# The last layer of an attention, expert and rational-layer kernel: its first products begun on two of three row tiles, and a fixed order of its instructions

## The chip, the cores and the metric

One core of one Trainium2 chip. The metric is the device time of one execution in microseconds. Before the change the median of 3 runs is 902.28 us (900.97 to 902.32).

## What is computed

Attention in which a query sees the keys of its own bucket, then a layer of 8 experts of which each token takes two, then a last layer with a rational activation:

```python
def _moe2_ref(x, w_in, w_out, a, b):      # x (1536, 512), w_in (512, 2048), w_out (2048, 512)
    h = x @ w_in
    h2 = h * h
    h3 = h2 * h
    P = a[0] + a[1] * h + a[2] * h2 + a[3] * h3
    Q = 1.0 + np.abs(b[0]) * np.abs(h) + np.abs(b[1]) * h2
    g = P / (Q + 1e-06)
    return (g @ w_out).astype(np.float32)
```

The change touches the last layer and its border to the last expert.

## The kernel before

The core's engines work from queues of their own: TensorE (PE) multiplies into PSUM, VectorE (DVE) and ScalarE (ACT) do the elementwise work and may read PSUM, GpSimd (POOL) works on SBUF alone and gathers rows by index, SyncE (SP) issues the other transfers. [...]

Each float32 factor is split in a high and a low part (fp32r), and a product is the sum of three terms: high x high, high x low, low x high.

**The last layer** (class `Last`) works through the 1536 tokens in 4 quarters of 384, each of three row tiles of 128 tokens. For each quarter there are 16 products f of 128 hidden columns, 64 in all, counted by q = 16 * quarter + f:
- `gather` (L1169) fetches a tile's two expert rows per token with two indexed transfers on GpSimd's queue; `combine` (L1178) adds them with their weights, one operation on ScalarE (L1180) and one on VectorE (L1181).
- `tr` (L1184) transposes the tile on TensorE (L1197) and splits it from PSUM into `x2T`: the high part on ScalarE (L1200), the low part on VectorE (L1201).
- `fc1` (L1203) is a first product: 12 matmuls (4 pieces of 128 rows by three terms) of 384 columns into one "ps1" bank (L1211).
- `first` (L1218): four ScalarE operations read the bank (L1222 to L1225: Abs into `ah`, the slope of Q into `qq`, a copy `hh`, the cubic term's start `uu`) and three VectorE operations work on those SBUF tiles (L1226 to L1228). `second` (L1230): 1/Q by Ln and Exp on ScalarE (L1233, L1234). `third` (L1236): three VectorE operations, a correction of 1/Q and the product with P (L1239 to L1241).
- `fourth` (L1243): the result is copied into the high half of `gT` by ScalarE (L1246) and GpSimd subtracts for the low half (L1247).
- `fc2` (L1250) is a second product: 9 matmuls of 512 columns (three terms by three row tiles) that add to three PSUM banks over a quarter's 16 values of f (L1263). Term (high, high) and the others come in the order term, row tile. At f = 15 the three banks are copied out (ScalarE L1274, VectorE L1272) and stored (L1276).

`run` (L1278) goes over steps s: first product s; `second` and `third` of s - 1; `fourth` and second product of s - 2; in the first three quarters the gathers of the next quarter's tiles at f = 4, 7, 10, and `combine` and `tr` two steps later; a weight split in every second step while weights are left (six of them). **The order** of the last layer's instructions on each engine is left to the scheduler of the framework, which uses its own estimates; the experts before it run in the order in which the program gives them (`manual_schedule`, for TensorE, ScalarE and VectorE).

`Weights.split` (L781) splits a weight tile of 1024 columns: high part on ScalarE (L793), low part on VectorE (L797); the next weight tile is then loaded on SP's queue.

**The border.** `Experts.run_last` (L1012) orders the last expert so that the rows of the first three tiles of the last layer can be gathered early, and does their `combine` and `tr` itself. Behind it stands `overflow_path` (L1104): all engines read a count and branch (L1108); the branch is not taken with these inputs. Only behind it do the first products of `Last.run` start, when all three tiles are there:

```python
        last.tr(1)
        for h in range(2):
            last.combine(2, slice(h * 256, h * 256 + 256))
        last.tr(2, 2)
```

Of the kernel before, what the change touches and what calls it, by code (L numbers as in the profile page):

```python
# [35 lines left out]
LONG = 3  # L36

# [702 lines left out]
class Weights:  # L740
# [5 lines left out]
    def __init__(self, tc, E):  # L746
        self.tc, self.nc, self.E = tc, tc.nc, E
        self.raw, self.slot = {}, {}
        self.ns = self.nl = 0
        self.ahead = 2  # L750
# [30 lines left out]
    def split(self, lo=None):  # L781
        nc, E = self.nc, self.E
        if self.ns >= 80:
            return
        n = self.ORDER[self.ns]
        self.ns += 1
        name = ("big1", "big2")[n // 8 % 2]
        pool = getattr(E, name)
        t = pool.tile([P, 2048], F32R, name=name, tag=name).rearrange("p (r s) -> p r s", r=2)
        self.slot[n] = t  # L790
        self.load()
        raw = self.raw.pop(n)
# [4 lines left out]
        (lo or nc.vector).tensor_tensor(t[:, 1, :], raw, t[:, 0, :].bitcast(F32), op=ALU.subtract)  # L797
        self.load()
# [59 lines left out]
class Experts:  # L858
# [153 lines left out]
    def run_last(self, last):  # L1012
# [3 lines left out]
        W = self.W  # L1016
# [26 lines left out]
        last.tr(0)  # L1043
# [60 lines left out]
def overflow_path(tc, E, last):  # L1104
# [3 lines left out]
    with tc.If(v > 0):  # L1108
# [3 lines left out]
        with tc.For_i(0, NE, 1) as e:  # L1112
            with tc.For_i(0, NTT, 1) as tt:
# [6 lines left out]
                ps = E.ps_1.tile([P, 512], F32, name="ps1")  # L1120
# [4 lines left out]
                for f in range(8):  # L1125
# [5 lines left out]
                    ph = E.ps_1.tile([P, 512], F32, name="ps1")  # L1131
# [22 lines left out]
        for tt in range(3):  # L1154
            last.gather(tt)
            last.combine(tt)
            last.tr(tt)


class Last:  # L1160
# [17 lines left out]
    def combine(self, tt, d=slice(0, DM)):  # L1178
        nc, E, t = self.nc, self.E, self.y[tt]
        nc.scalar.activation(t[:, 0, d], t[:, 0, d], AF.Copy, scale=E.gw[:, tt, 0:1])  # L1180
        nc.vector.scalar_tensor_tensor(t[:, 0, d], t[:, 1, d], E.gw[:, tt, 1:2], t[:, 0, d],  # L1181
                                       op0=ALU.mult, op1=ALU.add)

    def tr(self, tt, parts=1):  # L1184
# [6 lines left out]
        t, w = self.y[tt], 4 // parts  # L1191
        for h in range(parts):
            pool, name = ((E.ps_1, "ps1"), (E.ps_o, "o"))[(tt + h) % 2 if tt > 2 else 0]
            ps = pool.tile([P, 512], F32, name=name, tag=name)
# [8 lines left out]
    def fc1(self, q):  # L1203
# [4 lines left out]
        x = self.xT[ch]  # L1208
        ps = E.ps_1.tile([P, 512], F32, name="ps1")[:, 0:self.N]
        for n, (c, (a, b)) in enumerate([(c, t) for c in range(4) for t in ((0, 0), (0, 1), (1, 0))]):  # L1210
            nc.tensor.matmul(ps, w[:, a, c, fs], x[:, b, c, :], start=(n == 0), stop=(n == 11))  # L1211
        self.st[q] = {"ps": ps}
# [4 lines left out]

    def first(self, q):  # L1218
        nc, E, st = self.nc, self.E, self.st[q]
        ps = st.pop("ps")  # L1220
        ah, qq, u, h = (self.tmp(q, n, b) for n, b in (("ah", 1), ("qq", 2), ("uu", 2), ("hh", 1)))
        nc.scalar.activation(ah, ps, AF.Abs)  # L1222
        nc.scalar.activation(qq, ah, AF.Identity, scale=E.bb[:, 1:2], bias=E.bb[:, 0:1])  # L1223
        nc.scalar.activation(h, ps, AF.Copy)
        nc.scalar.activation(u, ps, AF.Identity, scale=E.na[:, 3:4], bias=E.na[:, 2:3])  # L1225
        nc.vector.tensor_mul(qq, qq, ah)  # L1226
        nc.vector.tensor_mul(u, u, h)  # L1227
        nc.vector.scalar_tensor_tensor(u, u, E.na[:, 1:2], h, op0=ALU.add, op1=ALU.mult)  # L1228

    def second(self, q):  # L1230
        nc, E, st = self.nc, self.E, self.st[q]
        r = self.tmp(q, "rr")
        nc.scalar.activation(r, st["qq"], AF.Ln, bias=E.c0)  # L1233
        nc.scalar.activation(r, r, AF.Exp, scale=-1.0)  # L1234
# [8 lines left out]
    def fourth(self, q):  # L1243
        nc, st = self.nc, self.st[q]
        g = self.pool.tile([P, 2, self.N], F32R, name="gT", bufs=2)
        nc.scalar.activation(g[:, 0, :], st["uu"], AF.Copy)  # L1246
        nc.gpsimd.tensor_tensor(g[:, 1, :], st["uu"], g[:, 0, :].bitcast(F32), op=ALU.subtract)  # L1247
        self.st[q] = g

    def fc2(self, q):  # L1250
# [9 lines left out]
        for a, b in ((0, 0), (0, 1), (1, 0)):  # L1260
            for j in range(3):
                ps = self.acc[ch][j]
                nc.tensor.matmul(ps, g[:, a, j * P:(j + 1) * P], w[:, b, f % 2, :],  # L1263
                                 start=(f == 0 and a + b == 0), stop=(f == 15 and a == 1))
# [13 lines left out]
    def run(self):  # L1278
        Q = 64
        for s in range(Q + 3):  # L1280
            ch, f = divmod(s, 16)
            if s < Q:
                self.fc1(s)
            if 0 <= s - 1 < Q:
                self.second(s - 1)
                self.third(s - 1)
            if 0 <= s - 2 < Q:
                self.fourth(s - 2)
            if s < Q:
                self.first(s)  # L1290
            if 0 <= s - 2 < Q:
                self.fc2(s - 2)
            if ch < 3:
                tt = 3 * (ch + 1)
                if f in (4, 7, 10):
                    self.gather(tt + (f - 4) // 3)
                if f in (6, 9, 12):
                    self.combine(tt + (f - 6) // 3)
                    self.tr(tt + (f - 6) // 3)
            if s % 2:  # L1300
                self.W.ahead = 2
                self.W.split()
# [3 lines left out]
def attention_moe_rational_kernel(ctx, tc, q, k, v, proj, w_gate, w_noise, noise, w1, w2, w_in, w_out, a, b, out):  # L1306
# [34 lines left out]
    with tc.tile_pool(name="big2", bufs=8) as E.big2, tc.tile_pool(name="xt", bufs=2) as E.xt:  # L1341
# [11 lines left out]
        with tc.tile_pool(name="fin", bufs=2) as last.pool:  # L1353
            last.run()
# [45 lines left out]
```

## Time and profile before

| what | value |
|---|---|
| median of 3 runs | 902.28 us |
| the profiled execution's own time | 905.34 us |
| its span (first to last instruction) | 903.6 us |
| TensorE busy | 863.3 us (96%) |
| VectorE busy | 747.9 us (83%) |
| ScalarE busy | 652.0 us (72%) |
| GpSimd busy | 357.8 us (40%) |
| mean granted TensorE clock | 0.986 |

The last expert ends, and the last layer starts, at about 604 us of the span. Busy time of TensorE is not TensorE at its peak: matmuls are pipelined, so the distance from one group's start to the next is what a group costs. A row of a timeline gives the start, the length, the engine, the line, the operation, the tiles out<-in, the shape, the count, and in brackets the idle time before it and what ended that. Some matmul records are missing from a trace, so counts can fall short.

### The profile page before, as it was taken

Reading aid. Unit: us, or ns where it says so; the run is one execution under the profiler, and the core shown is the slowest. Engines: PE = TensorE matmul, PEld = TensorE weight load, DVE = VectorE, ACT = ScalarE, POOL = GpSimd, SP = SyncE. Lnnn points to the kernel's source line nnn. Section 1 sums busy time; section 2 is a strip of 40 time slices with the busy share of each in tenths; the row PEclk is TensorE's granted clock in tenths of the full one; section 3 lists DMA queues with packets and bytes.
Section 4 is the critical chain, followed back from the end, with each engine's and each line's share of the span. In section 5 each row is a group of like instructions: output and inputs, shape, how many; then the busy total and the mean of one; then the engine's idle time right before and its main releaser. Section 6 shows DMA issues by size and latency. Waiting matters only on the chain. (4 is left out here: it accounts for less than half of the span.)

```text
span 903.6 us, 14378 instructions
## 1 busy us (share of the span) xinstructions
PE 863.3 (96%) x4673; PEld 769.6 (85%) x4673; DVE 747.9 (83%) x1450; ACT 652.0 (72%) x1272; POOL 357.8 (40%) x429
## 2 busy tenths in 40 slices
PE   7999999899998999999999999979999999999996
PEld 5999998799887888988998888868777999999895
DVE  6989999989896677867787667636999999999996
ACT  5898888788883555645656555527988988888885
POOL 5354445772465033534454343032672322222221
PEclk8999999999998999999999999998999999999999
DMA  6457776651152677797797877344231000000000
GB/s 203 115 129 202 207 204 192 179 174 32 50 198 102 187 234 251 262 292 258 267 325 227 281 235 252 128 123 148 82 91 32 30 12 27 10 1 19 18 1 35
DMA packets 90191, 131.39 MB, mean 145 GB/s; under 512 B 9248, under 2 KB 57376, under 8 KB 90112
## 3 DMA queue, kind: packets, MB, share of 16 engines
q1 hardware_dynamic: 86224, 117.72, 42.3%
q0 software_dynamic: 3888, 12.72, 4.3%
q8 instruction: 38, 0.62, 0.3%
q14 instruction: 41, 0.34, 0.1%
HBM read 87.68 MB, written 33.55 MB: 134 GB/s over the span
## 5 line engine op out<-in xcount | busy, mean ns | idle before, releaser
L923 PE MATMUL ps<-xsT,big 128*128 128x448 f32 (+1 forms) x768 | 159.2, 356 | 0.1
L1263 PE MATMUL s<-big,gT 128*128 128x512 f32 x528 | 141.0, 398 | 8.7 <-ACT gT L1246 5.6
L1211 PE MATMUL ps<-x2T,big 128*128 128x384 f32 x768 | 147.3, 340 | 1.5 <-DVEq L1108 1.5
L923 PEld LDWEIGHTS ps<-xsT,big 128*128 128x128 f32 x768 | 139.2, 189 | 7.9 <-DVE xsT L885 0.2
L1247 POOL TENSOR_TENSOR gT<-uu,gT 128x384 fp32r<-128x384 f32 x64 | 72.8, 1138 | 180.3 <-ACT gT L1246 150.8
L1211 PEld LDWEIGHTS ps<-x2T,big 128*128 128x128 f32 x768 | 137.2, 190 | 6.6 <-ACTq L1108 1.9
L943 PE MATMUL s<-big,hT 128*128 128x512 f32 x569 | 141.5, 393 | 0.7 <-ACT hT L928 0.7
L1263 PEld LDWEIGHTS s<-big,gT 128*128 128x128 f32 x528 | 96.3, 188 | 33.6 <-ACT gT L1246 9.8
L943 PEld LDWEIGHTS s<-big,hT 128*128 128x128 f32 x569 | 106.5, 188 | 21.3 <-ACT hT L928 1.0
L797 DVE TENSOR_TENSOR big<-wraw,big 128x1024 fp32r<-128x1024 f32 x76 | 97.4, 1286 | 27.8 <-ACT big L793 27.6
L357 DVE TENSOR_TENSOR PT<-ps,PT 128x384 fp32r<-128x384 f32 x192 | 105.4, 551 | 14.6 <-ACT PT L352 13.8
L847 POOL TENSOR_SCALAR convok<-convok 128x512 f32<-128x512 f32 x32 | 59.6, 1862 | 139.5 <-ACT convok L846 128.9
L352 ACT ACTIVATE PT<-ps 128x384 fp32r<-128x384 f32 x192 | 88.2, 493 | 29.8 <-PE ps L346 28.7
L338 ACT ACTIVATE probs<-s,sb 128x768 f32<-128x768 f32 x96 | 95.5, 995 | 3.6 <-DVE sb L331 3.4
L323 DVE TENSOR_REDUCE s<-s 128x1 f32<-128x768 f32 x96 | 92.2, 961 | 6.4 <-PE s L313 6.0
L313 PE MATMUL s<-big,qT 128*128 128x384 f32 x384 | 92.7, 364 | 4.1 <-ACT probs L338 3.2
L346 PE MATMUL ps<-ident,probs 128*128 128x128 f32 x576 | 85.7, 277 | 7.9 <-DVE sb L330 3.5
L793 ACT ACTIVATE big<-wraw 128x1024 fp32r<-128x1024 f32 x80 | 84.2, 1056 | 7.2 <-DMA wraw<-in_moe_w_dram 7.0
L367 PE MATMUL o<-PT,vhl 128*128 128x384 f32 x384 | 86.0, 346 | 0.6 <-ACT oT L373 0.6
L346 PEld LDWEIGHTS ps<-ident,probs 128*128 128x128 f32 x576 | 67.9, 141 | 20.2 <-PE ps L346 5.4
L1228 DVE SCALAR_TENSOR_TENSOR uu<-uu,na,hh 128x384 f32<-128x384 f32 x64 | 74.5, 1165 | 1.9
L928 ACT ACTIVATE hT<-ps 128x384 fp32r<-128x384 f32 x82 | 33.8, 412 | 51.9 <-PE ps L923 30.1
(222 smaller groups left out, 1474.9 us busy)
## 6 DMA issues: line engine op xcount, KB each, us to landing
wraw<-in_moe_w_dram SPq DMA_DIRECT2D x64, 512.0 KB, 5.4
wraw<-in_moe_w_in_dram SPq DMA_DIRECT2D x16, 512.0 KB, 5.6
wraw<-in_moe_w_out_dram SPq DMA_DIRECT2D x16, 512.0 KB, 4.1
xs<-zero SPq DMA_DIRECT2D x14, 512.0 KB, 4.4
qraw<-in_q_dram SPq DMA_DIRECT2D x32, 192.0 KB, 3.9
y<-io SPq DMA_DIRECT2D x24, 256.0 KB, 4.4
kraw<-in_k_dram SPq DMA_DIRECT2D x15, 384.0 KB, 4.0
w_in<-conv SPq DMA_DIRECT2D x16, 256.0 KB, 3.2
```

The costliest lines, as they stand in the source:

```text
L313: nc.tensor.matmul(ps[:, c, 0:384], T[:, r, q], R[:, r, c * 384:(c + 1) * 384], start=(r == 1), stop=(r == 0))
L323: nc.vector.tensor_reduce(m, ps[:, :, 0:384], axis=AX.XY, op=ALU.max, negate=True)
L338: nc.scalar.activation(pt.rearrange("p (c k) -> p c k", c=2), ps[:, :, 0:384], AF.Exp, bias=sb[:, 1:2], scale=sb[:, 0:1], accum_out=st["su ...
L346: nc.tensor.transpose(ps[:, i * P:(i + 1) * P], self.S[u]["P"][i][:, kt * P:(kt + 1) * P], E.ident)
L352: nc.scalar.activation(t[:, 0, :], ps[:, 0:384], AF.Copy)
L357: nc.vector.tensor_tensor(t[:, 1, :], ps[:, 0:384], t[:, 0, :].bitcast(F32), op=ALU.subtract)
L367: nc.tensor.matmul(self.O[u][:, 0:384], self.K[b, h]["vhl"][:, kt, :], t[:, r, :], start=(kt == 0 and r == 0), stop=(kt == 5 and r == 1))
L797: (lo or nc.vector).tensor_tensor(t[:, 1, :], raw, t[:, 0, :].bitcast(F32), op=ALU.subtract)
L923: nc.tensor.matmul(ps[:, 0:rows(e)], w[:, a, c, fs], x[:, c, b, 0:rows(e)], start=(n == 0), stop=(n == 11))
L943: nc.tensor.matmul(self.acc[e][j], h[a][:, j * P:(j + 1) * P] if j < 3 else tail, w[:, b, :], start=(f == 0 and a + b == 0), stop=(f == 7 ...
L1211: nc.tensor.matmul(ps, w[:, a, c, fs], x[:, b, c, :], start=(n == 0), stop=(n == 11))
L1263: nc.tensor.matmul(ps, g[:, a, j * P:(j + 1) * P], w[:, b, f % 2, :], start=(f == 0 and a + b == 0), stop=(f == 15 and a == 1))
```

## The change

1. Three first products begin before the third tile is there. In `run_last`, behind the second tile's transposes, product 0 is computed for tile 0 and for tile 1 separately and product 1 for tiles 0 and 1; then come the third tile's transposes, then product 2 for tiles 0 and 1. Behind the branch, `run` adds the third tile's columns of products 0, 1 and 2.
2. The last layer has a fixed order on TensorE, ScalarE and VectorE (`manual_schedule`). In step s TensorE does first product s + 1 and second product s - 3; `gT` has four buffers instead of two.
3. The elementwise work is cut anew. ScalarE: Abs with the slope from PSUM (`square`), the cubic term's start from PSUM (`cube`), Abs of Q's part, Ln, Exp, Copy: six operations where there were seven; the copies `ah` and `hh` go. VectorE: six operations as before, of which three read the PSUM bank as one input (`sign`, and both of `first`).
4. The low half of `gT` of the very last product is computed on VectorE, not on GpSimd. Second products at f = 0 and f = 15 go row tile by row tile.
5. Gathers at f = 0, 4, 8, their `combine` two steps later, `tr` at f = 5, 9, 13; weight splits from step 3 on, the low half at the end of VectorE's step.

```diff
@@ run_last
-        last.tr(0)
+        last.tr(0, (E.ps_1, "ps1"))
         last.combine(1)
 ...
-        last.tr(1)
+        last.tr(1, (E.ps_o, "o"))
         for h in range(2):
             last.combine(2, slice(h * 256, h * 256 + 256))
-        last.tr(2, 2)
+        for part in last.PARTS[:3]:
+            last.fc1(*part)
+        last.tr(2, (E.ps_o, "o"), (E.ps_s, "s"))
+        for part in last.PARTS[3:]:
+            last.fc1(*part)
@@ class Last
+    PARTS = (0, 0, 1), (0, 1, 2), (1, 0, 2), (2, 0, 2)
+    def fc1(self, q, i=0, j=3):
 ...
+        x, ps, n = self.xT[ch], self.st[q]["ps"], slice(i * P, j * P)
+        for k, (c, (a, b)) in enumerate([(c, t) for c in range(4) for t in ((0, 0), (0, 1), (1, 0))]):
+            nc.tensor.matmul(ps[:, n], w[:, a, c, fs], x[:, b, c, n], start=(k == 0), stop=(k == 11))
+    def square(self, q):
+        nc.scalar.activation(self.tmp(q, "qq"), st["ps"], AF.Abs, scale=E.bb[:, 1:2])
+    def sign(self, q):
+        nc.vector.scalar_tensor_tensor(st["qq"], st["qq"], E.bb[:, 0:1], st["ps"], op0=ALU.add, op1=ALU.mult)
+    def cube(self, q):
+        nc.scalar.activation(self.tmp(q, "uu"), st["ps"], AF.Identity, scale=E.na[:, 3:4], bias=E.na[:, 2:3])
     def first(self, q):
-        nc.scalar.activation(ah, ps, AF.Abs)
-        nc.scalar.activation(qq, ah, AF.Identity, scale=E.bb[:, 1:2], bias=E.bb[:, 0:1])
-        nc.scalar.activation(h, ps, AF.Copy)
-        nc.scalar.activation(u, ps, AF.Identity, scale=E.na[:, 3:4], bias=E.na[:, 2:3])
-        nc.vector.tensor_mul(qq, qq, ah)
-        nc.vector.tensor_mul(u, u, h)
-        nc.vector.scalar_tensor_tensor(u, u, E.na[:, 1:2], h, op0=ALU.add, op1=ALU.mult)
+        nc.vector.tensor_tensor(u, u, ps, op=ALU.mult)
+        nc.vector.scalar_tensor_tensor(u, u, E.na[:, 1:2], ps, op0=ALU.add, op1=ALU.mult)
     def second(self, q):
-        nc.scalar.activation(r, st["qq"], AF.Ln, bias=E.c0)
-        nc.scalar.activation(r, r, AF.Exp, scale=-1.0)
+        nc.scalar.activation(st["qq"], st["qq"], AF.Abs)
+        nc.scalar.activation(self.tmp(q, "rr"), st["qq"], AF.Ln, bias=E.c0)
+    def second2(self, q):
+        self.nc.scalar.activation(r, r, AF.Exp, scale=-1.0)
     def fourth(self, q):
-        g = self.pool.tile([P, 2, self.N], F32R, name="gT", bufs=2)
+        g = self.pool.tile([P, 2, self.N], F32R, name="gT", bufs=LAST + 1)
 ...
+        eng = nc.vector if q == 63 else nc.gpsimd
@@ fc2
+        for j, a, b in sorted(terms, key=lambda t: t[0]) if f in (0, 15) else terms:
@@ run
+            if rows and o == 0:
+                self.gather(tt)
+            for q in (0, 1) if s == 0 else (s + 1,):
+                if q < 3:
+                    self.fc1(q, 2, 3)
+                else:
+                    stage(self.fc1, q)
+            stage(self.square, s)
+            stage(self.sign, s)
+            stage(self.cube, s)
+            stage(self.third, s - 1)
+            stage(self.second, s)
+            stage(self.fc2, s - LAST)
+            if s < 2:
+                stage(self.fourth, s - 1)
+            if s % 2 and s > 1:
+                self.W.ahead = 2
+                self.W.split(False)
+            if rows and o == 2:
+                self.scale(tt)
+            stage(self.second2, s)
+            if s >= 2:
+                stage(self.fourth, s - 1)
+            stage(self.first, s)
+            self.W.low()
+            if rows and o == 2:
+                self.add(tt)
+            if ch < 3 and i and o == 1:
+                self.tr(tt - 1, (self.E.ps_o, "o"))
 ...
-            last.run()
+            with tc.manual_schedule(engines=MANUAL):
+                last.run()
```

`LAST` is 3; `i` and `o` are the quotient and remainder of f by 4, `tt` is 3 * (quarter + 1) + i, `rows` holds in the first three quarters for i < 3. First product 3 takes the bank "o", the others "ps1". In the branch that is not taken, other PSUM tiles are used and the four early pieces are computed again.

## Rows read from the trace of the kernel before

**Rows 1.** Busy time by stage: length, PE, PEld, DVE, ACT, POOL; clock, DMA.

```profile
607.80:614.60 6.80, 4.77 (x16) 4.28 (x17) 1.69 (x4) 0.77 (x2) 1.90 (x2) 0.50 0.29 64
624.70:690.00 65.30, 59.07 (x281) 48.10 (x280) 64.81 (x98) 56.85 (x109) 34.85 (x27) 1.00 0.24 71
690.00:830.00 140.00, 139.83 (x712) 126.44 (x713) 136.26 (x209) 121.94 (x244) 38.53 (x36) 1.00 0.05 16
```

**Rows 2.** Chain that ended last, middle of the last layer: start, length, what.

```profile
705.11 2.10 PE ps L1211 x12
707.21 2.08 PE s L1263 x9
```

**Rows 3.** Timeline of TensorE at the start of the last layer.

```profile
608.34 1.10 PE L1197 MATMUL ps<-ident,wraw 128*128 128x128 f32 x4 [3.85 <-DVE wraw L1181]
610.93 5.25 PE L1211 MATMUL ps<-x2T,big 128*128 128x384 f32 x19 [1.49 <-DVEq L1108]
...
624.74 1.57 PE L1211 MATMUL ps<-x2T,big 128*128 128x384 f32 x8
```

**Rows 4.** Timeline of ScalarE, the first activation of the last layer.

```profile
615.13 0.49 ACT L1222 ACTIVATE ah<-ps 128x384 f32<-128x384 f32 x1 [5.26 <-PE ps L1211]
```

**Rows 5.** Timeline of TensorE where matmuls have 128 columns: plain ones, then transposes.

```profile
279.66 0.87 PE L699 MATMUL s<-ident,kraw 128*128 128x128 f32 x6
...
635.50 0.60 PE L1197 MATMUL o<-ident,wraw 128*128 128x128 f32 x4
635.86 0.60 PE L1211 MATMUL ps<-x2T,big 128*128 128x384 f32 x2
```

**Rows 6.** Groups, 624.7 to 690 us: busy us, mean ns, idle before, releasers.

```profile
L1263 PE MATMUL s<-big,gT 128*128 128x512 f32 x118 | 32.3, 410 | 6.1 <-ACT gT L1246 3.2 <-POOL gT L1247 2.9
```

**Rows 7.** Waits, 891 to 904 us: us in total, times, longest.

```profile
PE s L1263 <- ACT gT L1246: 2.1, 2, 1.6
```

**Rows 8.** Timeline of VectorE: low parts of the second and third tile.

```profile
605.16 0.69 DVE L1201 TENSOR_TENSOR x2T<-ps,x2T 128x512 fp32r<-128x512 f32 x1 [0.84 <-ACT x2T L1200]
...
609.45 0.87 DVE L1201 TENSOR_TENSOR x2T<-ps,x2T 128x256 fp32r<-128x256 f32 x2 [0.82 <-ACT x2T L1200]
```

**Rows 9.** Timeline of all engines in an expert: two engines on one PSUM bank.

```profile
549.52 0.55 DVE L929 SCALAR_TENSOR_TENSOR hT<-ps,hT 128x384 fp32r<-128x384 f32 x1
...
550.11 0.23 ACT L928 ACTIVATE kept<-ps 128x64 fp32r<-128x64 f32 x1 [1.38 <-DVE hT L929]
```

**Rows 10.** Timeline of ScalarE in the last layer's middle.

```profile
702.28 0.62 ACT L1233 ACTIVATE rr<-qq,c 128x384 f32<-128x384 f32 x1
702.92 0.53 ACT L1234 ACTIVATE rr<-rr 128x384 f32<-128x384 f32 x1
703.36 0.47 ACT L1222 ACTIVATE ah<-ps 128x384 f32<-128x384 f32 x1
...
705.03 0.67 ACT L1225 ACTIVATE uu<-ps,na 128x384 f32<-128x384 f32 x1
```

**Rows 11.** VectorE lines L357 (attention) and L1228 (690 to 890): ns min/median/max.

```profile
L357 DVE TENSOR_TENSOR PT<-ps,PT x192: 528/549/559, 18.7 to 276.9; 128x384 fp32r<-128x384 f32 x192
...
L1228 DVE SCALAR_TENSOR_TENSOR uu<-uu,na,hh x48: 619/1260/1351, 690.1 to 888.3; 128x384 f32<-128x384 f32 x48
```

**Rows 12.** GpSimd's groups: subtraction, 690 to 830 us; gathers, 624.7 to 690.

```profile
L1247 POOL TENSOR_TENSOR gT<-uu,gT 128x384 fp32r<-128x384 f32 x34 | 37.1, 1090 | 102.9 <-ACT gT L1246 87.5 <-PE o L1197 6.3 <-issue 5.8
...
L1173 POOL DMA_INDIRECT wraw<-y,slot x14 | 17.6, 1261 | 7.9 <-DVE qq L1226 3.6 <-issue 1.8 <-PE ps L1197 1.7
```

**Rows 13.** ScalarE's groups, 624.7 to 690 us: weight splits and row tiles.

```profile
L1180 ACT ACTIVATE wraw<-wraw,gw 128x512 f32<-128x512 f32 x8 | 5.7, 712 | 0.0
L793 ACT ACTIVATE big<-wraw 128x1024 fp32r<-128x1024 f32 x5 | 5.3, 1057 | 0.0
...
L1200 ACT ACTIVATE x2T<-o 128x512 fp32r<-128x512 f32 x2 | 1.2, 590 | 0.0
```

More of the change, by code (lines that the diff above doesn't have):

```diff
@@ L749, in __init__ @@
         self.ns = self.nl = 0
+        self.left = None
         self.ahead = 2
@@ L796, in split, with low @@
             self.tc.keep_in_program_order(r)
-        (lo or nc.vector).tensor_tensor(t[:, 1, :], raw, t[:, 0, :].bitcast(F32), op=ALU.subtract)
-        self.load()
+        self.left = t, raw
+        if lo is not False:
+            self.low(lo)
+    def low(self, eng=None):
+        if self.left:
+            t, raw = self.left
+            self.left = None
+            (eng or self.nc.vector).tensor_tensor(t[:, 1, :], raw, t[:, 0, :].bitcast(F32), op=ALU.subtract)
+            self.load()
 class Narrow:
@@ L1156, in overflow_path @@
             last.combine(tt)
-            last.tr(tt)
+            last.tr(tt, (E.ps_o, "o"))
+        for part in last.PARTS:
+            last.fc1(*part)
 class Last:
@@ L1190, in tr @@
             self.xT[ch] = t.rearrange("p (r c n) -> p r c n", r=2, c=4)
[L1191 to L1194, printed above, removed]
+        t, w = self.y[tt], 4 // len(rooms)
+        for h, (pool, name) in enumerate(rooms):
+            ps = pool.tile([P, 2, 512] if name == "s" else [P, 512], F32, name=name, tag=name)
+            ps = ps[:, 0, :] if name == "s" else ps
             for c in range(w):
@@ L1207, in fc1 @@
         fs = slice(f % 2 * P, f % 2 * P + P)
[L1208 to L1212, printed above, removed]
+        if q not in self.st:
+            pool, name = (E.ps_o, "o") if q == 3 else (E.ps_1, "ps1")
+            self.st[q] = {"ps": pool.tile([P, 512], F32, name=name, tag=name)[:, 0:self.N]}
+        x, ps, n = self.xT[ch], self.st[q]["ps"], slice(i * P, j * P)
+        for k, (c, (a, b)) in enumerate([(c, t) for c in range(4) for t in ((0, 0), (0, 1), (1, 0))]):
+            nc.tensor.matmul(ps[:, n], w[:, a, c, fs], x[:, b, c, n], start=(k == 0), stop=(k == 11))
     def tmp(self, q, name, bufs=2):
@@ L1259, in fc2 @@
                 self.acc[ch][2] = E.ps_o.tile([P, 512], F32, name="o")
[L1260 to L1264, printed above, removed]
+        terms = [(j, a, b) for a, b in ((0, 0), (0, 1), (1, 0)) for j in range(3)]
+        for j, a, b in sorted(terms, key=lambda t: t[0]) if f in (0, 15) else terms:
+            nc.tensor.matmul(self.acc[ch][j], g[:, a, j * P:(j + 1) * P], w[:, b, f % 2, :],
+                             start=(f == 0 and a + b == 0), stop=(f == 15 and a == 1))
         if f == 15:
@@ L1279, in run, with stage @@
         Q = 64
+        def stage(f, q):
+            if 0 <= q < Q:
+                f(q)
         for s in range(Q + 3):
             ch, f = divmod(s, 16)
[L1282 to L1300, printed above, removed]
-                self.W.ahead = 2
-                self.W.split()
+            i, o = divmod(f, 4)
+            tt = 3 * (ch + 1) + i
+            rows = ch < 3 and i < 3
+            if rows and o == 0:
[14 more added lines that the diff above has]
+            if s % 2 and s > 1:
+                self.W.ahead = 2
+                self.W.split(False)
[10 more added lines that the diff above has]
+                self.tr(tt - 1, (self.E.ps_o, "o"))
 @with_exitstack
```

33 lines of the change are left out of this document (20 added, 13 removed).

## Prediction

> **What bounds the kernel now.** I read the busy time by stage first, then the chain that ended last, TensorE's own timeline around the change, and the waits. From 690 us on TensorE is the bound: it is busy for 139.83 of 140 us at a granted clock of 1.00 [rows 1], and the chain only alternates 12 first products in 2.10 us with 9 second products in 2.08 us [rows 2]. One step of the last layer so costs 4.19 us, and nothing done on other engines can shorten it. The losses lie before and after that stretch:
> - Start. After the second tile's transposes TensorE is idle until 608.34, for 3.85 us [rows 3]. [...]
> - First quarter. Between 624.74 [rows 3] and 690.17 TensorE does 12 first products, 13 second ones and three groups of transposes. At 2.10, 2.08 and 0.43 us (0.36 between starts [rows 5], and a slower restart) that is 53.6 us, so some 11.8 us are lost. VectorE is busy 64.81 of 65.3 us there [rows 1], and TensorE waits for ScalarE's and GpSimd's halves of gT, 6.1 us of plain idle time [rows 6].
> - End. TensorE waits twice for the last gT, 2.1 us [rows 7], and some 0.5 us go in restarts: 2.6 us.
>
> **The change part by part.**
>
> *Early products.* Product 0 is cut into three pieces of one row tile (128 columns), products 1 and 2 into pieces of two tiles and one. No row shows such a narrow first product. The nearest are 128-column matmuls of other kinds: 4 transposes in 0.36 us, or 0.09 each, and 6 plain ones in 0.87 us, or 0.145 each with the last one's drain [rows 5]. I take 0.11 between them, so 1.3 us for a piece of 12. If nothing overlapped, a piece could cost 0.27 us per instruction (the drain of one, an estimate from the 0.60 us of 4 transposes less three of their starts), 3.3 us; below 0.09 I see no reason to go. For two tiles the steps of 0.175 (384 columns) and 0.231 (512) [rows 2] extrapolate to 0.12, or 1.45 us.
> The second tile is in SBUF at 605.85 [rows 8]. Piece 1 runs from 604.5 to 605.85, piece 2 to 607.2, product 1's two tiles to 608.7. The third tile's transposes, ready at 608.34, so start 0.3 late; their last copy moves from 610.32 [rows 8] to 610.6, and product 2's two tiles fit beneath it. TensorE still passes the all-engine branch, where the first product now follows VectorE's copy by 0.6 us [rows 3, 8]; so the third-tile pieces start at 611.2, and ScalarE has product 0 at 612.75 instead of 615.13. No idle time near 3.85 us is left ahead of it, so I count full clock.
>
> *One elementwise step in the fixed order.* ScalarE and VectorE now read one PSUM bank in turn. The trace shows such turns: ScalarE's 64-column activation starts at 550.11, 0.04 us after VectorE's read of the same bank ends [rows 9]. So the third activation (cube) waits for VectorE's product (sign). ScalarE's chain from one step to the next [rows 10]: Abs with a scale 0.56 (0.47, and 0.09 for the scale operand, an estimate), hand-over 0.05, VectorE 0.55, hand-over 0.05, cube 0.60 (its 0.67 less 0.07 of overlap), Abs 0.54 (as Exp), Ln 0.64 with Exp behind it, Exp and Copy 0.43 each to the next start: **3.85 us**, below TensorE's 4.19. ScalarE has six activations in a step where it had seven.
> VectorE has 6 operations, three with a PSUM input at 0.55 us each, as L357 [rows 11], and three between 0.56 and 0.62: 3.4 us. Before, the worst one (L1228) took 1.26 in the median instead of 0.62 [rows 11], since it met GpSimd's subtraction of 1.09 us [rows 12]; with ScalarE's copy last in the step, that subtraction falls beside VectorE's PSUM reads. L357, with one PSUM input, stayed at 528 to 559 ns through all 192 executions, while GpSimd worked beside many of them.
> [...] The rows differ: 549 ns with PSUM against 619 ns, the fastest L1228.
>
> *First quarter.* TensorE now issues product s+1 and second product s-3 in step s. ScalarE starts step 1 at 612.75 + 3.42 (no Copy yet) = 616.2. The first gT is copied at 619.7, GpSimd has its low half at 620.95, and TensorE, which can do only two matmuls before that, ends second product 0 at 622.6, with five first products done. Before, this point was 624.74: **2.1 us gained**.
> Steps 1 to 13 cost ScalarE 13 x 3.85 = 50.0, plus six weight splits (1.06, 0.95 from start to start) and three row tiles (0.71 and 0.59, 1.09 so counted) [rows 13]: 9.0. So step 14 begins at 675.2, and second product 12, whose gT is copied at the end of step 13, at 675.0. TensorE alone would be there at 622.6 + 12 x 2.105 + 11 x 2.083 + 1.3 = 672.1. The loss is **2.95 instead of 11.8 us, 8.85 gained**. From there ScalarE is quicker than TensorE, and three steps of room (gT with four buffers) take up the copies at a quarter's end, 1.2 us.
>
> *End.* After the last first product TensorE has four second products ahead of the last, 8.3 us; the last gT with its low half on VectorE needs 7 us. So both waits go: **2.6 us**. The last quarter's result is ordered by row tile, so one of the two copies of some 0.6 us (as a tile's 0.59 [rows 13]) that ScalarE makes back to back moves ahead: **0.6 us**.
>
> *At nothing.* The gathers stay at two issues per tile, at steps 0, 4, 8 instead of 4, 7, 10, in GpSimd's queue ahead of the subtraction: 1.26 us each [rows 12], and 2.5 + 1.1 us fit in a step of 4.19; without that cover a gT would be 2.5 us late. The six weight loads on SP's queue have 10 us before their first split in step 3. The low half of a split on VectorE moves behind the products, hidden by 0.4 us of idle time per step; without it sign would be late next. The last low half, moved from GpSimd, is in the 7 us.
>
> **Sum:** 2.1 + 8.85 + 2.6 + 0.6 = 14.1 us. The profiled execution took 905.34 us, span 903.6, so its span would be 889.5; it is 3.1 over the median, 902.28, from which I subtract the same: **888.2 us**.
>
> **Rivals.**
> *Better: TensorE never waits after its first second product.* ScalarE's chain would need to be 3.6 us, with no cost for hand-overs or the scale operand. Another 2.95, and 0.5 for narrow products at 0.09: 884.7. Against it: the hand-over is there [rows 9].
> *Dear pieces.* At 0.27 us per narrow instruction the transposes of tile 3 start at 613 to 614 and the third-tile pieces follow: ScalarE begins up to 10 us later, 892 to 898. The transposes are then queued behind the very work meant to fill their wait. For it: nothing in the trace has this form; against: narrow matmuls of other kinds overlap [rows 5].
> *The early pieces do nothing*, as the branch, not the third tile, holds the products and the clock falls anyway: minus the 2.1, and the rest stays: 890.3.
> *Slower: GpSimd's subtraction meets VectorE's third group.* The three operations of the step before still read two SBUF tiles. If the subtraction runs 0.2 us or more beyond the 1.1 us I have for it, 0.64 us (1.26 against 0.62) come onto them in each step; sign waits behind them on VectorE, cube behind sign, and the next step behind those. VectorE's step becomes 3.4 + 0.64, with its idle wait for Abs 4.12 us, and TensorE no longer sets the pace: from 616.2, 63 x 4.12, some 22 us of splits, tiles and copies on VectorE (like ScalarE's [rows 13]), and 9.3 for the last gT, product and stores make a span of 907.1, in time 905.8. It decides from 4.06 us per step on. For it: L1228's median bears this mark. Against: by my order the subtraction ends as the group begins.
> [...]
>
> **How the numbers follow.** A measurement here can tell 0.2%, 1.8 us, from no change. Chances: forecast 0.60; never waits 0.10; early pieces do nothing 0.08; dear pieces 0.10; slower 0.12, of which 0.04 for a milder meeting that only takes the gain back. The likeliest case's own range is 885 to 892. To hold 8 in 10 with the unknown prices I take 884.0 to 898.5, from the better case to the dear pieces; the slower case is left out. Faster: 0.60 + 0.10 + 0.08 + 0.10 = 0.88; same 0.04; slower 0.08.
>
> **What would show it.** Right: the clock at 1.00 from 604 to 620; product 0 with ScalarE near 612.8; VectorE's PSUM readers at 0.55 whatever GpSimd does; TensorE idle some 3 us between 625 and 690, and not in the end. Wrong: a step above 4.19 us in the middle, bounded by VectorE or ScalarE; the third group's operations at 1.2 us; narrow pieces over 2 us; a wait in front of the third tile's transposes that the pieces caused.

## The result and the profile after

The changed kernel takes 895.51 us in the median (894.74 to 897.92, 5 runs) beside 902.32 us (900.97 to 905.68, 5 runs) of the kernel before: a ratio of 0.9904, 95% interval 0.9877 to 0.993. So 6.8 us were gained where 14.1 were forecast.

Executions also differ ahead of the change: the second tile's transposes, where the change begins, start at 603.87 us in the profile before and at 601.72 after, and in the profiles of the experiments below between 600.38 and 607.08. Within the profiles I therefore count from these transposes (their first start, to the end of the span): 299.7 us before (903.6 less 603.87) and 291.5 after (893.2 less 601.72), **8.2 us less**. This count repeats better than the run times: e3 and e9 below, the same kernel, give 288.4 and 288.9 by it, while the five run times of e3 alone lie between 890.54 and 894.03 us.

TensorE's timeline at the start of the last layer, after (against [rows 3]):

```profile
601.72 0.66 PE L1222 MATMUL o<-ident,wraw 128*128 128x128 f32 x4 [0.26 <-DVE wraw L1206]
602.13 4.58 PE L1242 MATMUL ps<-x2T,big 128*128 128x128 f32 x36
606.54 0.38 PE L1222 MATMUL o<-ident,wraw 128*128 128x128 f32 x2
606.76 0.38 PE L1222 MATMUL s<-ident,wraw 128*128 128x128 f32 x2
606.90 1.67 PE L1242 MATMUL ps<-x2T,big 128*128 128x256 f32 x12
611.26 7.26 PE L1242 MATMUL ps<-x2T,big 128*128 128x128 f32 x36 [2.69 <-PEq L1124]
618.32 4.09 PE L1242 MATMUL o<-x2T,big 128*128 128x384 f32 x12
622.25 2.25 PE L1242 MATMUL ps<-x2T,big 128*128 128x384 f32 x12
```

The early pieces do what they should: 36 narrow matmuls (24 of 128 columns, 12 of 256) from 602.13 to 606.54, 0.12 us each in the mean, and no idle time of 3.85 us any more. But behind product 2's two tiles TensorE now waits 2.69 us for its own sequencer (PEq) at L1124, the branch around the overflow path; the 36 narrow matmuls behind that wait take 7.26 us where the 36 ahead of it took 4.58, and product 3 then takes 4.09 us, twice its 2.1. The windows say why (columns as in [rows 1]):

```profile
604.00:608.00 4.00, 4.00 (x36) 4.00 (x36) 1.50 (x4) 1.57 (x4) 0.95 (x2) 1.00 0.50 125
608.00:612.00 4.00, 1.30 (x12) 1.13 (x11) 0.14 (x1) 0.00 (x0) 0.88 (x2) 1.00 0.21 45
612.00:622.00 10.00, 10.00 (x44) 10.00 (x43) 5.70 (x10) 6.37 (x12) 4.69 (x5) 0.50 0.76 263
690.00:830.00 140.00, 140.00 (x716) 126.81 (x714) 122.41 (x215) 111.82 (x217) 35.76 (x35) 1.00 0.05 16
```

TensorE is busy throughout to 608; then it idles at the branch, and from 612 to 622 the granted clock is 0.50: the low stretch of [rows 1] has not gone but moved back, and grown from 6.8 to 10 us. The last row is as before: TensorE bound, full clock.

The branch itself, by engine, after, and then TensorE's in the kernel before (count, ns min/median/max, start):

```profile
L1124 PEldq COMPARE_BRANCH  x1: 3772/3772/3772, 607.3 to 607.3; - x1
L1124 ACTq COMPARE_BRANCH  x1: 50/50/50, 607.7 to 607.7; - x1
L1124 DVEq COMPARE_BRANCH  x1: 72/72/72, 608.3 to 608.3; - x1
```

```profile
L1108 PEldq COMPARE_BRANCH  x1: 352/352/352, 609.4 to 609.4; - x1
```

Only TensorE's branch is long; ScalarE's and VectorE's take 50 and 72 ns. ScalarE's timeline (against [rows 4, 10]); the row at 613.57 is step 0, the one at 617.02 step 1, the last one step 14:

```profile
613.57 0.58 ACT L1251 ACTIVATE qq<-ps,bb 128x384 f32<-128x384 f32 x1 [5.95 <-PE ps L1242]
614.83 0.67 ACT L1259 ACTIVATE uu<-ps,na 128x384 f32<-128x384 f32 x1 [0.68 <-DVE qq L1255]
615.40 0.51 ACT L1269 ACTIVATE qq<-qq 128x384 f32<-128x384 f32 x1
...
617.02 0.56 ACT L1251 ACTIVATE qq<-ps,bb 128x384 f32<-128x384 f32 x1
...
675.34 0.51 ACT L1286 ACTIVATE gT<-uu 128x384 fp32r<-128x384 f32 x1
675.75 0.58 ACT L1225 ACTIVATE x2T<-o 128x512 fp32r<-128x512 f32 x1
676.23 0.57 ACT L1251 ACTIVATE qq<-ps,bb 128x384 f32<-128x384 f32 x1
```

ScalarE has product 0 at 613.57, 11.85 us after the transposes; before it was 615.13, 11.26 us after them. It starts **later**, by 0.6 us. From that start to the end 279.6 us pass (893.2 less 613.57) where it was 288.4 (299.7 less 11.26). TensorE between step 14 and the second quarter, and the groups of VectorE from 690 to 890 us (against [rows 11]):

```profile
676.38 0.44 PE L1242 MATMUL ps<-x2T,big 128*128 128x384 f32 x1 [0.71 <-ACT x2T L1225]
677.11 2.18 PE L1242 MATMUL ps<-x2T,big 128*128 128x384 f32 x11 [0.28 <-DVE x2T L1226]
679.13 2.24 PE L1305 MATMUL s<-big,gT 128*128 128x512 f32 x9
...
695.88 1.30 PE L1305 MATMUL s<-big,gT 128*128 128x512 f32 x5
```

```profile
L1281 DVE SCALAR_TENSOR_TENSOR uu<-uu,na,rr 128x384 f32<-128x384 f32 x48 | 29.7, 619 | 1.7
L1265 DVE SCALAR_TENSOR_TENSOR uu<-uu,na,ps 128x384 f32<-128x384 f32 x47 | 28.9, 615 | 1.7
...
L1264 DVE TENSOR_TENSOR uu<-uu,ps 128x384 f32<-128x384 f32 x47 | 25.7, 547 | 0.0
```

VectorE's slow operation of 1260 ns is gone; the same operation with one PSUM input (L1265) and with two SBUF inputs (L1281) takes 615 and 619 ns.

### The profile page after: what moved, and what is told of

Same layout as the page of the kernel before. It is cut to its first block, busy times and chain, and to the rows that moved or that the text cites. A ratio compares the mean times of both kernels' runs of the same rounds, so it can differ in the third digit from the quotient of the medians.

```text
span 893.2 us, 14461 instructions
## 1 busy us (share of the span) xinstructions
PE 861.5 (96%) x4721; PEld 773.7 (87%) x4721; DVE 713.4 (80%) x1451; ACT 625.5 (70%) x1208; POOL 350.3 (39%) x428
## 5 line engine op out<-in xcount | busy, mean ns | idle before, releaser
L1242 PE MATMUL ps<-x2T,big 128*128 128x384 f32 (+2 forms) x804 | 150.8, 337 | 4.4 <-PEq L1124 2.7
L1242 PEld LDWEIGHTS ps<-x2T,big 128*128 128x128 f32 x804 | 139.8, 193 | 11.0 <-issue 2.9
L1289 POOL TENSOR_TENSOR gT<-uu,gT 128x384 fp32r<-128x384 f32 x63 | 65.4, 1038 | 184.8 <-ACT gT L1286 162.1
L1305 PE MATMUL s<-big,gT 128*128 128x512 f32 x528 | 137.0, 393 | 0.0
L858 POOL TENSOR_SCALAR convok<-convok 128x512 f32<-128x512 f32 x32 | 63.1, 1972 | 134.7 <-ACT convok L857 131.4
L1259 ACT ACTIVATE uu<-ps,na 128x384 f32<-128x384 f32 x63 | 42.4, 672 | 48.2 <-POOL gT L1289 37.6
```

What stands on the lines that cost most here:

```text
L1242: nc.tensor.matmul(ps[:, n], w[:, a, c, fs], x[:, b, c, n], start=(k == 0), stop=(k == 11))
L1305: nc.tensor.matmul(self.acc[ch][j], g[:, a, j * P:(j + 1) * P], w[:, b, f % 2, :], start=(f == 0 and a + b == 0), stop=(f == 15 and a == 1))
```

## The experiments

Two things fall short: the start, where ScalarE is 0.6 us later instead of 2.4 sooner (615.13 to 612.75), and the stretch from step 0 to the end. My theory for the first was that TensorE's branch waits for its own code. The path not taken now recomputes the early pieces (48 matmuls and their weight loads, 96 instructions), so that TensorE jumps further:

```diff
@@ overflow_path, in the body that is not taken
         for tt in range(3):
             last.gather(tt)
             last.combine(tt)
-            last.tr(tt)
+            last.tr(tt, (E.ps_o, "o"))
+        for part in last.PARTS:
+            last.fc1(*part)
```

Counted from zero in TensorE's compiled program, the branch stands at instruction 6766 with its target at 7033 before, and at 6860 with 7221 after. (The expectations below count the next branch, which stands three instructions on and inside the path: 6863 for 6860. The theories don't depend on these three.) All results in one table: TensorE's branch; ScalarE's step 0 and the end of the span, both counted from the second tile's transposes; the ratio to the kernel before with its 95% interval.

```
kernel               branch  step 0    end  ratio
before                 0.35   11.26  299.7
changed                3.77   11.85  291.5  0.9904 [0.9877, 0.9930]
e1 short path          3.80   12.54  292.3  0.9892 [0.9869, 0.9915]
e2 +92 ahead           0.35    9.31  288.9  0.9869 [0.9846, 0.9892]
e3 loop in the path    0.35    8.76  288.4  0.9860 [0.9836, 0.9883]
e4 no early pieces     0.35   11.79  291.3  0.9909 [0.9877, 0.9941]
e5 +10 ahead           2.81   11.06  290.6  0.9883 [0.9856, 0.9909]
e6 before, +94 ahead   3.42   13.12  301.7  1.0023 [1.0003, 1.0043]
e7 fourth bank         2.87   10.41  309.7  1.0134 [1.0110, 1.0158]
e8 fourth bank apart   0.35    9.32  292.5  0.9919 [0.9887, 0.9950]
e9 e3 again            0.35    9.39  288.9  0.9879 [0.9852, 0.9907]
e10 early row tile     0.35    8.69  288.4  0.9860 [0.9829, 0.9891]
e11 e10 and a bank     0.24    9.38  289.1  0.9853 [0.9824, 0.9883]
e12 bank alone         0.35    9.35  288.9  0.9859 [0.9830, 0.9888]
```

**The branch: e1 to e4.** Four kernels on one chip. e1, a shorter path:

```diff
-        for part in last.PARTS:
-            last.fc1(*part)
```

> Leaves out the recomputation of the early pieces in the overflow path that is not taken (48 matmuls, 96 instructions with their weight loads), so what TensorE's branch jumps over is again about as long as before; all that runs is unchanged. Block theory (TensorE's branch of 3.77 us waited for a block of its own instructions, which the longer path had pushed out of reach): the branch falls below 0.5 us, the third-tile pieces start near 609 instead of 611.26 us, the granted clock stays at 1.00 from 611 to 622, and about 5.9 us come off: 889.6 us (888 to 891.5). Drain theory (the branch waits until the 36 early pieces are through the array, however long the path): the branch stays near 3.8 us and the time near 895.5 us. Length theory (a jump over more than some 300 instructions is slow wherever it stands): as the block theory.

Measured: the branch takes 3.80 us, and nothing is gained. My arithmetic of the borders failed, since I had put them at multiples of 256 from the program's first instruction. The other three say where they are.

e2, only the warm-up at the kernel's start, 600 us earlier:

```diff
-    for i in range(WARM):
-        tc.nc.tensor.matmul(ps, z[:, 0:P], z, start=True, stop=True)
+    for i in range(56):
+        tc.nc.tensor.matmul(ps[:, 0:92], z[:, 0:P], z[:, 0:92], start=True, stop=True)
```

> The changed kernel whole, the path not taken as long as it is; only the 10 warm-up matmuls of 512 columns at the kernel's start become 56 of 92 columns (5152 columns for 5120), which puts 92 more instructions ahead of the branch and so moves where it and its target lie against the blocks of 256 instructions. Block theory: before, branch and target lay 1 border apart, in the changed kernel 2; moved by 92 they lie 1 apart again, so the branch is below 0.5 us and the time 889.6 us (888 to 891.5). Length theory and drain theory: nothing is changed for them, the branch stays near 3.8 us and the time near 895.5 us.

Measured: branch 0.35 us with the path as long as in the changed kernel, and no wait. TensorE's timeline, then a window in the columns of [rows 1]:

```profile
609.68 1.67 PE L1242 MATMUL ps<-x2T,big 128*128 128x256 f32 x12
611.50 4.21 PE L1242 MATMUL ps<-x2T,big 128*128 128x128 f32 x36
615.54 2.30 PE L1242 MATMUL o<-x2T,big 128*128 128x384 f32 x12
```

```profile
608.00:622.00 14.00, 12.82 (x89) 11.48 (x88) 7.76 (x15) 7.33 (x15) 6.47 (x6) 1.00 0.61 189
```

The third-tile pieces follow at once, the clock stays at 1.00, and the end comes 2.6 us sooner than in the changed kernel (288.9 for 291.5), not 5.9. Length theory and drain theory fall: path and pieces are the same.

e3, the path rewritten shorter:

```diff
-                for f in range(8):
+                nc.vector.memset(x[:, 0, :], 0.0)
+                with tc.For_i(0, 8, 1) as f:
...
-                    nc.tensor.matmul(acc[:, 0, :], h, w2[:, 0, :], start=(f == 0), stop=(f == 7))
-                nc.vector.tensor_copy(x[:, 0, :], acc[:, 0, :])
+                    nc.tensor.matmul(acc[:, 0, :], h, w2[:, 0, :], start=True, stop=True)
+                    nc.vector.tensor_tensor(x[:, 0, :], x[:, 0, :], acc[:, 0, :], op=ALU.add)
...
-        for part in last.PARTS:
-            last.fc1(*part)
+        for q in range(3):
+            last.fc1(q, 0, 2)
```

> The path not taken is rewritten shorter without leaving anything out: its eight slices of hidden rows become a loop of one slice (VectorE adds the slices up), and it recomputes the early products as three of two tiles rather than four pieces; 217 instructions to jump over on TensorE instead of 358. What runs is unchanged. Block theory and length theory: branch below 0.5 us, 889.6 us (888 to 891.5). Drain theory: 895.5 us.

Measured: branch 0.35 us, 288.4 us, ratio 0.986; 3.1 us sooner than the changed kernel by the count from the transposes.

e4, no early pieces:

```diff
-        for part in last.PARTS[:3]:
-            last.fc1(*part)
         last.tr(2, (E.ps_o, "o"), (E.ps_s, "s"))
-        for part in last.PARTS[3:]:
-            last.fc1(*part)
...
-                    self.fc1(q, 2, 3)
+                    self.fc1(q)
```

> The changed kernel without the early pieces: the first three products are whole ones behind the branch; the fixed order and VectorE reading PSUM stay; the path not taken recomputes no products. Block theory: the branch is short; TensorE idles before it, so product 0 runs at half clock from about 608.8 to 613.0 us and ScalarE starts near 613, 0.6 us sooner than in the changed kernel, with products 1 and 2 at full clock behind it; fc2 of step 0 about 2 us sooner: 893.6 us (892 to 895.5), so that in the changed kernel the early pieces cost more than they give. A rival by which the early pieces are what the measured gain came from: 2 us or more slower than the changed kernel, 897.5 us or above.

Measured: ScalarE's step 0 at 11.79 us and the end at 291.3 us, as good as the changed kernel (11.85, 291.5), and not the 2 us better that I expected. TensorE waits 4.61 us for the third tile there, and its granted clock is 0.50 from 604 to 612. So the early pieces, as they stand in the changed kernel, neither give nor cost: what they save in waiting for the third tile goes into the branch and the half clock behind it. Without the stall they are worth 2.4 to 2.9 us (291.3 less 288.9 and 288.4). The 8.2 us that were gained come from the rest of the change, the fixed order, the new elementwise step and the new end together; no run takes these apart.

**The place of the branch: e5 and e6.** TensorE's instruction fetches are a DMA queue of their own. After, over the whole kernel; then in the stretch of TensorE's branch, 607.2 to 611.1, and behind it, 611.1 to 613:

```profile
q8 instruction: 39, 0.64, 0.3%
...
q8 instruction: 1, 0.02, 2.3%
...
q8 instruction: 1, 0.02, 4.1%
```

A fetch is 16.4 KB. The 39 fetches bring TensorE's whole compiled program of 10004 instructions (the kernel before: 38 for 9811), so some 256 each. In the changed kernel one fetch falls into the branch (it starts at 608.26 us and takes 1.47; the branch runs from 607.26 to 611.03) and the next comes right behind it (611.77). In e2 one lies between 600 and 602.2 us, long ahead of the branch at 610.1, and none falls into it. In the long branches of the changed kernel and of e5 (below) a fetch starts 1.0 and 0.2 us into the branch, which ends 1.3 and about 1.5 us after that fetch is over; in the kernel before, where the branch takes 0.35 us, it ends at 609.75 and the next fetch starts at 610.52. e1 to e4 fit borders every 256 instructions with one between 6861 and 6869: the jumps of the changed kernel (6860 to 7221) and of e1 (6860 to 7125) cross two, those of before (6766 to 7033), e2 (6952 to 7313), e3 (6860 to 7080) and e4 (6764 to 7029) one. e1 and e3 have the branch at the same place and differ in the target alone: 3.80 against 0.35 us.

e5 is the changed kernel with 15 warm-up matmuls of 341 columns.

> The changed kernel with only the warm-up at its start cut otherwise: 15 matmuls of 341 columns for 10 of 512, so 10 instructions more ahead of the branch, no more. If the first four runs are explained by borders of 256 instructions, all of them together put a border between instruction 6864 and 6869 of TensorE's program (counted from its first one), and the next 256 further. The branch, at 6863 in the changed kernel with its target at 7221, has two borders to cross; at 6873 with its target at 7231 it has one. Block theory: TensorE's branch takes below 0.5 us instead of 3.77, ScalarE begins step 0 some 2.6 to 3.1 us sooner after the second tile's transposes (11.85 us in the changed kernel), and from those transposes to the end 288.3 to 288.9 us pass instead of 291.5; ratio to before about 0.987. Length theory (a jump this long is slow) and a theory by which the 92 instructions of the second run helped in another way (a warmer array, another start): branch 3.8 us, 291.5 us, ratio 0.990.

Measured: 2.81 us, between what the theories said, and so a miss; ScalarE 0.8 us sooner than in the changed kernel, the end 0.9. The branch, at 6870, has just passed the border ahead of it, and the fetch shows between 613.4 and 616.3 us, during the branch, which starts at 613.5. One border alone doesn't make a jump cheap: 2.81 us here, 0.35 in e2 to e4. In e2 the fetch lies over 7 us ahead of the branch, here it starts 0.2 us into it; that the target's block had not come yet is my inference. I had left that out.

e6 is the kernel before with 57 warm-up matmuls of 90 columns, so that its branch stands at 6860 and its target at 7127:

> The kernel before, with nothing but its warm-up cut into 57 matmuls of 90 columns: 94 more instructions ahead of its branch, which then stands at 6863 with its target at 7126, where the first of these runs had them. Block theory: the kernel before gets the stall too: TensorE's branch takes 3.8 us instead of 0.35, the first product starts 2 to 3 us later after the second tile's transposes than 7.07 us, and from those transposes to the end 301.7 to 302.7 us pass instead of 299.7; ratio to before 1.002 to 1.0035. Rival by which only the early pieces make the branch long: 299.7 us, branch 0.35 us, ratio 1.000.

Measured: branch 3.42 us, 301.7 us, 2.0 more than before; ratio 1.0023. The wait, in the columns engine, line, releaser, us in total, times, longest:

```profile
PE ps L1211 <- PEq L1108: 4.0, 1, 4.0
```

So the stall needs none of the change: 94 instructions more in the first 5 us bring it into the old kernel at 609 us.

**Behind step 14: e7 to e12.** In all kernels with the new order but e7 and e8, 279.5 to 279.8 us lie between step 0 and the end, whatever the start was. The forecast comes to 276.7: 288.4 less 11.7, which is the 14.1 less the 2.4 us by which step 0 was to start sooner. In the rows above, product 16 starts at 676.38 and second product 12 at 679.13, 2.9 us after step 14 begins, where I had it 0.2 ahead. I first held that product 16 lacks a PSUM bank (the kernel has three tiles "ps1" and one "o" of one bank, 512 columns, and two result tiles "s" of two).

e7, with e5's warm-up, put the products 7, 11 and 15 of each quarter into the unused half of a result tile:

```diff
+            spare = f in (7, 11, 15)
+            room = self.spare[ch] if spare else pool.tile([P, 512], F32, name=name, tag=name)
...
             self.acc[ch] = [two[0][:, 0, :], two[1][:, 0, :], two[0][:, 1, :]]
+            self.spare[ch] = two[1][:, 1, :]
```

> The fifth run's kernel with a fourth PSUM bank for products: in each quarter the products 7, 11 and 15 go into the half of the result tile that no row tile uses, so product 16 needs not wait until VectorE has read product 13. Bank theory (what was over-forecast behind ScalarE's 14 steps is product 16, which TensorE issues ahead of second product 12 and which waits for a bank): second product 12 starts 1.8 us sooner after the second tile's transposes than in the fifth run, and so does the end: 286.5 to 287 us instead of 288.3 to 288.9; ratio to before 0.985. Rival (the copy of gT and its low half set second product 12 anyway): no difference from the fifth run.

Measured: 19 us longer than e5, and no answer. One tile now holds a product and a result, and the result's matmuls wait until ScalarE has read the product:

```profile
647.15 3.61 PE L1308 MATMUL s<-big,gT 128*128 128x512 f32 x8 [6.32 <-ACT uu L1261]
```

The run shows one thing more. Its branch took 2.87 us, with 1.84 us of idle time, and the granted clock behind it stayed at 1.00; in e5 1.76 us of idle time were followed by a clock of 0.50 from 620 to 624 us. So whether a stall of this length also costs the clock stays open.

e8 takes that order away (the two lie in different banks), on e3:

```diff
+            if j == 1:
+                for r in self.reads[-10:]:
+                    self.tc.declare_no_dep(m.ins, r.ins, reason="other bank")
```

> The third run's kernel (short path not taken, nothing left out) with the fourth PSUM bank of the seventh run, and with what spoilt that run taken away: there the products 7, 11 and 15 shared a tile with one result, so second products waited for ScalarE's reading of a product that they do not touch (6.3 us the longest); here those orders between different banks are not asked for. Bank theory: second product 12 starts 72.5 us after the second tile's transposes instead of 74.36 in the third run, and the end comes 286.5 instead of 288.33 us after them; ratio to before 0.2% below that of the third run's kernel in the same call. Rival (gT and its low half set second product 12 anyway): 74.36 and 288.33 again, same ratio.

> The third run's kernel once more, beside the eighth on one chip: branch 0.35 us, 288.3 us from the second tile's transposes to the end, ratio to before 0.986 to 0.988.

Measured: e9 repeats e3 (branch 0.35, 288.9 with a start 0.6 us later). e8 is 3.6 us longer and again no answer, for another reason: GpSimd's order is not written by hand, and it came out with four gathers ahead of one subtraction, so that the cubic's first activation waited 3.06 us for it (behind it 11 matmuls of product 16 took 3.48 us, from 676.39, where the changed kernel's take 2.18):

```profile
665.51 1.11 POOL L1194 DMA_INDIRECT wraw<-y,slot  x1
666.93 0.95 POOL L1194 DMA_INDIRECT wraw<-y,slot  x1 [0.30 <-issue]
668.18 0.95 POOL L1194 DMA_INDIRECT wraw<-y,slot  x1 [0.31 <-ACT gT L1299]
669.43 1.14 POOL L1194 DMA_INDIRECT wraw<-y,slot  x1 [0.30 <-issue]
670.60 1.00 POOL L1302 TENSOR_TENSOR gT<-uu,gT 128x384 fp32r<-128x384 f32 x1
```

```profile
671.63 0.67 ACT L1271 ACTIVATE uu<-ps,na 128x384 f32<-128x384 f32 x1 [3.06 <-POOL gT L1302]
```

The rows of the result then gave another theory: product 16 waits for `x2T`, the third row tile of the next quarter, which ScalarE and VectorE copy only at the end of step 13. e10 transposes it one step sooner and holds GpSimd's order; e11 adds a bank for product 15; e12 has the bank alone, on e3.

```diff
-            if ch < 3 and i and o == 1:
+            if ch < 3 and i and (s == 12 or o == 1 and s != 13):
```

```diff
+            spare = q == 15
```

> The third run's kernel with the third row tile of the next quarter transposed and copied in step 12 instead of 13, in the first quarter alone; GpSimd's order is kept as it was. In the ninth run product 16 waited for that tile's copies (0.71 us ahead of it and 0.4 us behind its first matmul), when its PSUM bank had been free for 1.25 us. Tile theory (that wait is what product 16, and so second product 12, lost): second product 12 1.1 us sooner after the second tile's transposes than in the third and ninth run (74.36 and 74.98 us), the end likewise, 287.2 to 287.9 us instead of 288.3 to 289.0; ratio to before 0.1% lower. Bank theory (VectorE's reading of product 13 holds it): no difference.

> The tenth run's kernel with product 15 in a fourth PSUM bank, so that product 16 takes the bank of product 12. If tile and bank hold product 16 one behind the other: second product 12 starts up to 1 us sooner than in the tenth run, end 286.2 to 287.9 us after the second tile's transposes. If the tile alone holds it: as the tenth run.

> The third run's kernel with product 15 in a fourth PSUM bank and nothing else; GpSimd's order is that of the third run, which in the eighth run it was not (four gathers stood ahead of one subtraction). Tile theory: no difference from the third and ninth run, end 288.3 to 289.0 us after the second tile's transposes. Bank theory: 1.8 us sooner.

Measured, from step 0 so that the different starts drop out: second product 12 starts at 65.6 us in the changed kernel (679.13 less 613.57) and in e12, at 64.5 in e10 and at 63.7 in e11. So the tile holds product 16, and the bank behind it, as the tile theory has it. But the end does not move: 288.4, 289.1 and 288.9 us, all 279.6 or 279.7 behind step 0. e11's TensorE shows where its lead of 1.9 us is lost, at product 19 and at second product 16, the first of the second quarter:

```profile
685.53 2.35 PE L1250 MATMUL ps<-x2T,big 128*128 128x384 f32 x12 [0.62 <-DVE uu L1281]
687.71 2.24 PE L1322 MATMUL s<-big,gT 128*128 128x512 f32 x9
...
692.94 2.31 PE L1322 MATMUL s<-big,gT 128*128 128x512 f32 x9 [0.87 <-DVE io L1335]
```

Product 19 waits 0.62 us until VectorE has read the bank that it takes. Second product 16 waits 0.87 us for VectorE's copy of the first quarter's result, whose bank it needs. Second product 15 is over at 689.79, but VectorE begins that copy at 692.11, behind four operations of step 18. It begins it 81.4 us behind step 0 in the changed kernel (694.95 less 613.57) and 81.5 in e10 and e11, whatever TensorE's lead, and second product 16 starts 82.3 us behind step 0 in all three (695.88 less 613.57). TensorE's own chain and VectorE's end there within some hundredths of a microsecond in the changed kernel, so shortening the one gains nothing. Whether moving the result copies ahead in step 18, together with e11, brings the 3 us was not tried.

The best versions are e3 and e11, 0.9860 and 0.9853 of the kernel before, which their intervals do not tell apart. e3 was ahead of e1, which has the stall, on the same chip: 892.28 against 895.67 us in the median.

## Why the prediction was right in direction and short in size

The gain that was forecast was 5.9 us more than the profiles show (14.1 against 8.2), in two steps. The measured 895.51 us lies in the range of 884.0 to 898.5, but outside the likeliest case's own, 885 to 892; the range reached so far up for the dear pieces, which did not come. That it holds is in part luck.

**The start, 3.0 us short.** Right: the price of the pieces (0.12 us for 0.11 and 0.12), the third tile's transposes 4.8 us behind the second's (forecast 4.8), no idle time ahead of them. The step that failed is "TensorE still passes the all-engine branch, where the first product now follows VectorE's copy by 0.6 us", and with it "so I count full clock". I took the 0.6 us over to a branch that I had not costed, although the change puts 94 instructions ahead of it and 96 into the path it jumps over. It cost 2.69 us of idle time and then half clock from 612 to 622. e2 and e3 remove the stall and leave the last layer's work as it is, and they have step 0 at 9.31 and 8.76 us, where the forecast had 8.88 (612.75 less 603.87).

The runs fit a wait for the branch's own code: by the fitted borders the branch takes 0.35 us with the target one border on (before, e2, e3, e4), 3.42 to 3.80 us with it two on (the changed kernel, e1, e6), and 2.81 and 2.87 in e5 and e7, where the border ahead of the branch had just been passed. What the engine waits for within the branch is my inference from these times and from the fetches; no run shows it by itself.

The rival "the early pieces do nothing, as the branch holds the products and the clock falls anyway" came true at the start in what it says of the gain (e4: 291.3 against 291.5 us); that the branch would wait for its own code was not in it. Its 890.3 us priced the loss at 2.1 us, where the start came 3.0 later than forecast, and the second shortfall was not in it.

**Step 0 to the end, 2.9 us short.** Right: ScalarE's chain. From step 1 to step 14 it took 59.21 us (676.23 less 617.02), forecast 13 x 3.85 + 9.0 = 59.05; Abs with a scale, an estimate of 0.56 us, took 564 ns in the mean (L1251, 624.7 to 690 us). Right too: the PSUM readers did not slow beside GpSimd. L1255 took 603 to 617 ns in its 64 executions, 57 of which overlap GpSimd's subtraction (one at 644.37 us, 0.62 long, beside the one from 644.00 to 645.01), and L1264, which does not meet it, 543 to 554. Nor did the PSUM source itself cost: 615 ns with one (L1265), 619 without (L1281). The end went as forecast: from second product 16 to the end of the span 197.3 us (893.2 less 695.88), forecast 197.7 (889.5 less 675.0, 4 steps of 4.19 off). The step that failed is "second product 12 ... at 675.0", and behind it "three steps of room ... take up the copies at a quarter's end". TensorE issues product 16 ahead of second product 12, and that one waits for the row tile's copies made at the end of step 13; I counted the tile's time on ScalarE and not who waits for it. And second product 16 needs a bank that the result copies give back, which VectorE reaches only behind four operations of step 18. Second product 16 was forecast 79.0 us behind step 0 (675.0 + 16.75 less 612.75) and came at 82.3.

The other rivals fell: no dear pieces, no meeting in the third group (619 ns for L1281), and TensorE did wait in the first quarter (it is busy for 63.98 of 65.66 us from 624.34 to 690). The price of the dear pieces held a slip: 0.60 us less three starts of 0.09 is 0.33 us for an instruction, not 0.27, so that case would have been dearer than written.

## What to carry to other kernels

TensorE's branch around a path that never runs took 0.24 to 0.35 us or 2.81 to 3.80 here, by where it and its target lie in the engine's program: compare the branch instruction's own length on every engine before and after, and shorten the untaken path (e3: a loop, fewer recomputed pieces) or shift it (e2: 92 instructions more in the warm-up); ten instructions more, in e5, were not enough. Work that fills a wait gains only if what comes next is ready too; look for the next releaser at that place before counting the idle time as gained. Where a stage hands over (the last tile of a quarter, the copies that free its banks), list who is queued behind each copy, not only what the copy costs its own engine.

## What was not expected of the hardware

- The length of TensorE's branch changes from 0.35 to 3.4 us through 94 instructions 600 us earlier (e6), with all else the same, and to 2.81 us rather than 0.35 when the border is passed just ahead of it (e5).
- In e8 the displaced subtraction (670.60 to 671.60 us) ran beside VectorE's third operation on two SBUF tiles, which took 1.64 us instead of 0.62, the meeting that the slower rival feared:

```profile
670.38 1.64 DVE L1294 SCALAR_TENSOR_TENSOR uu<-uu,na,rr 128x384 f32<-128x384 f32 x1
```
